# Half-size products for pairs of ff tiles in batches 1 to 3, with one set of keys and queries and a new order of steps

## The chip, the core and the metric

The kernel runs on one core of a Trainium2 chip. The core has a matrix engine (TensorE, "PE" in the profile, with its weight loads as a row of their own, "PEld"), a vector engine (VectorE, "DVE"), an activation engine (ScalarE, "ACT"), a general engine (GpSimd, "POOL") and SyncE ("SP"), which here only issues transfers. Each engine works through its own queue in order and waits on semaphores of the others. PE writes into PSUM, eight banks of 2 KB per partition; all other tiles lie in SBUF. The metric is the device time of one execution in microseconds (us), lower is better; times of several runs are given as a median. Inputs are drawn once and are the same in all runs.

## What is computed

A sparse attention followed by a two-layer network, for 4 batches of 768 positions with 8 heads of 64:

```
k_sum, v_sum = max / mean of k, v over blocks of 32 positions
scores = scale * q k^T, kept where |i - j| < 16, beside scale * q k_sum^T + log(32)
attn   = softmax(scores) [v ; v_sum]            # (4, 8, 768, 64) -> x (3072, 512)
h      = x @ w_in                               # 512 -> 2048
g      = h * sigmoid(1.702 h)
out    = g @ w_out                              # 2048 -> 512
```

## The kernel before

The program is one long list of steps, the string `ORDER`. Each word names a step with its arguments; a step calls a small function that issues the step's instructions, each on a fixed engine, and every engine runs its instructions in the order of the words (`_Ordered`, so that all instructions have line 28 in the profile). A last letter a, d or g names the engine of a step: ACT, DVE or POOL. The order is written out by hand or by a planner outside the file; there is no scheduler in it. The work of a batch:

- **Loads and keys.** `lk`, `lq`, `lv` issue the loads of keys, queries and values on POOL. For batch 0 and 1 keys and queries are turned on PE; for batches 2 and 3 `xk` and `xq` turn them by transposing transfers on SP. `xa` is DVE's maximum over key blocks, `ka` and `kR` copy halos and block rows. `kxs` and `qTs` are two sets of keys and queries, used in turn (`b % 2`); set 0 lies in the pool `even`. `vw` are two sets of values.
- **Attention.** `s` scores (PE), `e` exponent (ACT), `m` mask (DVE), `v` values (PE), `nn` normalisation (DVE). Then `d`, a transposing transfer on SP, brings x into `xTT[half][g]` (half of the positions, half of d_model). It is interleaved with the products of the batch before.
- **ff.** `f.half.nt.k0123.bank`: four matmuls of 128x128 by 128x384 add up one of 16 tiles of h for one half in a bank; `g.half.nt`: gelu on ACT into `gTb[:, nt, half]`. 32 such tiles per batch.
- **Sums and products.** The second layer is already done with half-size blocks, seven products in place of eight: `gs.j.n.w` are four kinds of sums (w = 0 to 3) of blocks of g for n tiles from j, 16-bit tensors; `ws.w.part` the same for w_out, once. `p.t.w` is product w = 1 to 7 for position tile t = 0 to 2, eight matmuls of 256 columns each. Products 1, 2 and 4 take g as it is, 5, 6, 7 and 3 take sums 0, 1, 2 and 3. `x.t.w` takes a finished product out of its bank, on ACT or DVE; `o` stores to DRAM on SP.
- **Others.** `vm`, `vb` block sums of values, `sd`, `ha` transfers of halos of values, `gate.n` a small POOL copy that holds POOL's later loads back until values of a batch are in place, `G` and `X` load ACT's tables.

Functions for seven products in the first layer exist (`w_sum7`, `x_sum7`, `product7`, `taken7`, `gelu7`), but `ORDER` calls only `P7.0`, which closes the pool `even` and opens nothing. PSUM is used as four single banks (0 to 3) and two double ones (`4x`, `5x`; a third digit 0, 1 or 2 is first half, second half or both).

Of the kernel before, what the change touches and what calls it, by code (L numbers as in the profile page):

```python
# [17 lines left out]
class _Ordered:  # L18


    def __init__(self, tc, eng):
        self._tc, self._eng = tc, eng

    def __getattr__(self, name):
        f = getattr(self._eng, name)

        def call(*a, **kw):
            r = f(*a, **kw)  # L28
            self._tc.keep_in_program_order(r)
            return r  # L30

        return call
# [23 lines left out]
qc.1.a gs.6.1.3 lv.2.0.0 tq.2.42 p.1.1.3 qc.2.a gs.7.1.1 gs.4.2.3 p.0.5.1 x.0.5.a p.0.6 tq.3.52 kr.0.1.d s.1.0.0.42
x.0.6.a x.0.2.a gs.7.1.2 X gs.7.1.3 kr.1.1.d x.1.1.d xm.3.1 kh.2.1.g p.1.2.0 e.0.0 p.0.3 p.0.7 lq.2.3 m.0.0 x.0.3.a
x.0.7.a kh.1.1.d qc.3.d s.1.1.0.42 e.1.0 p.1.6 xm.2.1 vm.1.42 o.0.0.0.0.2 s.1.0.1.52 lv.2.5.0 e.0.1 kr.2.1.g kh.3.1.d
p.0.4 vb sd.1.1.0 x.0.4.a gate.1 s.1.1.1.52 e.1.1 lv.2.3.0 p.1.5.1 kr.3.1.d x.1.5.d x.1.2.a m.1.0 x.1.6.a s.1.0.2.52
sd.1.0.0 p.2.1.2 m.0.1 x.2.1.a p.1.3 s.1.0.3.42 o.0.0.1.0.2 p.1.7 lv.2.1.1 e.0.2 m.1.1 lk.2.0 e.0.3 s.1.1.2.52 lk.2.2  # L60
lv.2.2.0 x.1.7.a x.1.3.a lv.2.2.1 lk.2.3 p.2.6 e.1.2 lv.2.5.1 s.1.1.3.42 m.0.2 p.1.4 v.1.0.0.50 e.1.3 v.1.0.1.51 lk.2.1
m.0.3 m.1.3 lk.2.4 v.1.1.0.40 v.1.1.1.41 x.2.6.a p.2.5.1 G lk.2.5 nn.0.0 nn.1.0 x.2.5.a lk.2.7 p.2.7 o.0.1.0.0.2
t.0.0.52 lk.2.6 x.2.7.a x.1.4.a p.2.2.3 t.1.0.42 p.2.3 x.2.2.a c.0.0.a c.1.0.a m.1.2 lv.2.1.0 v.1.0.2.50 lq.2.1
v.1.0.3.51 v.1.1.2.40 x.2.3.a v.1.1.3.41 p.2.4 f.0.1.k01.0 nn.0.1 t.0.1.52 nn.1.1 lv.2.0.1 c.0.1.d o.0.1.1.0.2 lq.2.4
lv.2.3.1 x.2.4.a o.0.2.0.0.2 f.0.9.k01.3 f.0.8.k01.1 f.0.0.k01.2 lv.2.4.0 t.1.1.42 c.1.1.d f.0.1.k23 g.0.1 f.0.8.k23
f.0.0.k23 g.0.8 g.0.0 f.0.9.k23 o.0.2.1.0.2 g.0.9 lq.2.6 lv.2.4.1 xk.0.0.0 lq.2.5 f.1.1.k0123.0 f.1.0.k0123.2 lq.2.7
g.1.0 xk.0.0.1 g.1.1 f.1.8.k0123.1 lv.3.1.0 xk.0.1.0 g.1.8 xk.0.1.1 f.1.9.k0123.3 f.0.2.k0123.2 g.1.9 g.0.2
f.1.2.k0123.1 lk.3.0 f.1.10.k0123.3 g.1.2 f.0.10.k0123.0 f.1.3.k0123.1 xq.0.0 gs.0.2.0 g.1.10 g.1.3 g.0.10
f.1.11.k0123.3 f.0.3.k0123.2 f.0.11.k0123.0 g.1.11 g.0.3 f.1.12.k0123.3 gs.0.2.2.d xq.0.1 g.0.11 gs.0.2.1.g
f.0.4.k0123.2 f.1.4.k0123.1 g.0.4 xa.0.0 f.0.12.k0123.0 g.1.4 f.0.5.k0123.2 f.1.5.k0123.1 g.0.12 lk.3.4 g.1.12  # L70
f.0.13.k0123.0 f.1.15.k0123.3 g.0.5 f.0.6.k0123.2 g.1.5 g.0.13 lv.3.1.1 g.1.15 vm.2.42 f.0.14.k0123.0 gs.2.2.0 ka.0.g vb
f.1.6.k0123.1 lk.3.2 g.0.14 g.0.6 lk.3.7 f.1.13.k0123.3 lk.3.3 gs.2.2.1 f.0.15.k0123.0 gs.2.2.3 lk.3.5 g.1.6 ha.2.2.0
g.1.13 f.1.7.k0123.2 f.1.14.k0123.3 lv.3.4.1 f.0.7.k0123.1 g.1.7 xa.1.0 gs.7.1.0 sd.2.0.0 kR.0.d g.0.15 lv.3.0.1
sd.2.1.0 g.1.14 gs.4.2.0 p.0.2.0 s.2.0.0.42 gs.6.1.0 ha.2.0.0 g.0.7 gs.7.1.2 s.2.0.1.52 lv.3.5.0 gs.4.2.1 X lv.3.2.0
p.2.5.1 p.0.1.2 e.0.1 gs.7.1.1 gs.7.1.3 ha.2.3.0 gs.6.1.1 x.0.1.d p.0.5.3 x.0.2.a x.0.5.d e.0.0 m.0.0 s.2.0.2.42
gs.6.1.2.d gs.6.1.3 ha.2.1.0 s.2.0.3.52 gs.4.2.2.d e.0.2 e.0.3 gs.0.2.3 p.1.5.0 p.0.6 gs.4.2.3 gs.2.2.2.d s.2.1.0.42
s.2.1.1.52 x.0.6.a lk.3.1 p.0.3 p.0.7 e.1.0 x.0.3.a lv.3.3.0 m.0.3 lq.3.0 p.1.1.3 x.0.7.a e.1.1 lq.3.4 m.0.1 s.2.1.3.52
m.0.2 s.2.1.2.42 x.1.1.a e.1.3 e.1.2 p.0.4 p.1.6 lv.3.0.0 x.0.4.a v.2.0.0.40 x.1.6.a v.2.0.2.50 v.2.0.1.41 x.1.5.d
v.2.0.3.51 m.1.2 p.1.2.2 m.1.1 lq.3.5 p.1.7 o.1.0.0.0.2 nn.0.0 x.1.2.a o.1.0.1.0.2 m.1.3 x.1.7.a p.1.3 nn.0.1 lv.3.3.1
lq.3.7 m.1.0 p.1.4 p.2.1.2 v.2.1.0.40 v.2.1.2.50 d.0.0 v.2.1.1.41 v.2.1.3.51 x.2.5.a x.2.1.d x.1.3.a lq.3.3 p.2.6  # L80
o.1.1.0.0.2 x.1.4.d d.0.1 p.2.3 nn.1.0 x.2.6.a p.2.7 nn.1.1 p.2.2.3 x.2.7.a x.2.2.a lv.3.4.0 d.1.0 lv.3.2.1 p.2.4
f.0.9.k01.3 x.2.3.a f.0.1.k01.0 G d.1.1 o.1.2.0.0.2 f.0.1.k23 f.0.8.k01.1 f.0.8.k23 f.0.9.k23 x.2.4.a f.0.0.k01.2
f.0.0.k23 lk.3.6 g.0.1 g.0.9 g.0.8 f.1.1.k0123.0 f.1.8.k0123.1 g.0.0 f.1.9.k0123.3 g.1.1 g.1.9 g.1.8 f.1.0.k0123.2
f.0.10.k0123.0 g.0.10 gate.2 g.1.0 gs.0.2.2 xk.1.1.0 f.1.2.k0123.1 gs.0.2.0.d gs.0.2.1 xk.1.0.1 f.1.10.k0123.3 g.1.2
o.1.1.1.0.2 g.1.10 lq.3.6 f.0.2.k0123.2 gs.0.2.3 lv.3.5.1 f.1.3.k0123.1 vm.3.52 g.1.3 xk.1.1.1 g.0.2 xk.1.0.0
o.1.2.1.0.2 f.0.13.k0123.0 f.0.3.k0123.2 f.1.11.k0123.3 f.0.12.k0123.1 g.0.3 g.0.13 g.1.11 xa.0.1 f.0.4.k0123.2 xq.1.1
f.1.12.k0123.3 lq.3.1 f.0.11.k0123.0 g.0.4 gs.2.2.2.g g.0.12 f.1.5.k0123.1 g.0.11 lq.3.2 vb xa.1.1 xq.1.0 f.0.5.k0123.2
# [12 lines left out]
f.1.13.k0123.3 g.1.2 f.1.3.k0123.1 g.0.10 f.0.3.k0123.2 g.1.13 f.1.10.k0123.3 g.0.3 f.0.11.k0123.0 f.0.4.k0123.2 g.1.3  # L100
# [13 lines left out]
def kernel(  # L114
# [633 lines left out]

    seven = {}

    def seven_pool(n):
        even.close()
        if not n:
            return
# [209 lines left out]
```

## Time and profile before

| | us |
|---|---|
| median of 3 runs | 212.25 |
| lowest, highest | 211.74, 213.11 |
| the profiled execution, whole | 211.7 |
| its span in the trace | 210.0 |

All rows of a profile come from the profiled execution. Its span runs from the first to the last instruction; the remaining 1.7 us lie around it. PE's mean granted clock was 0.996. Engines' busy times are unions, so pipelined instructions count once. A timeline row gives start, length, engine, line, operation, what it writes and reads, and how many like instructions are merged in it; in brackets the idle time before it and what ended it. In rows of groups, "busy, mean ns" is followed by the idle time of the engine before these instructions.

### The profile page before, as it was taken

How to read it: one execution, taken by the hardware profiler on the slowest of the kernel's cores; microseconds unless marked ns; L12 is line 12 of the kernel's file. 1: busy time of each engine (PE TensorE's matmuls, PEld its weight loads, DVE VectorE, ACT ScalarE, POOL GpSimd, SP SyncE). 2: the span in 40 equal slices, each digit the busy share in tenths (PEclk: the TensorE clock that was granted, in tenths of full speed). 3: DMA queues.
4: the chain of work that ended last, by engine and by line, in shares of the span. 5: the costliest groups of instructions: out<-in, count | busy, mean ns of one | idle time of the engine just before them, and what ended most of it. 6: DMA issues, size and time to landing. Idle time of an engine off the chain costs nothing.

```text
span 210.0 us, 5880 instructions
## 1 busy us (share of the span) xinstructions
PE 200.4 (95%) x2440; PEld 145.8 (69%) x2440; DVE 130.8 (62%) x311; ACT 114.3 (54%) x227; POOL 109.1 (52%) x157
## 2 busy tenths in 40 slices
PE   7998798999999999999999999999999999999993
PEld 5656554667887886556788865657888865668882
DVE  5577873798997871168997822694888500166342
ACT  2473885659666736676764336567670157671100
POOL 7999972399982998448949422431000000863000
PEclk9999999999999999999999999999999999999998
DMA  4999999999999999999999999939215920000214
GB/s 67 162 166 189 209 213 221 182 144 122 99 134 199 156 177 183 130 126 141 148 166 204 142 227 180 187 29 169 50 53 139 160 105 0 0 3 0 100 53 150
DMA packets 96458, 27.74 MB, mean 132 GB/s; under 512 B 85024, under 2 KB 93488, under 8 KB 96432
## 3 DMA queue, kind: packets, MB, share of 16 engines
q0 software_dynamic: 70800, 13.64, 82.7%
q1 hardware_dynamic: 25632, 13.74, 33.2%
q8 instruction: 19, 0.31, 0.6%
q14 instruction: 7, 0.06, 0.1%
HBM read 27.26 MB, written 6.29 MB: 160 GB/s over the span
## 4 chain that ended last, share of the span: by engine, by line
PE 79%; POOL 12%; DMA 5%; issue 1%; DVE 1%; SPq 0%; POOLq 0%; DVEq 0%
PE ph L28 36%; PE poA L28 19%; PE poB L28 10%; PE poC L28 5%; PE ps_s L28 3%; PE ps_av L28 3%; DMA vw<-vw 2%; POOL mk L28 2%; DMA out_dram<-osb 2%; POOL v0n L28 2%; POOL w_in_sb L28 2%; POOL kb L28 2%; POOL kx L28 2%; POOL qb L28 1%; PE ps_t L28 1%
## 5 line engine op out<-in xcount | busy, mean ns | idle before, releaser
L28 PE MATMUL ph<-xT,w_in_sb 128*128 128x384 f16 x512 | 86.1, 326 | 0.4 <-DVE osb L28 0.4
L28 ACT ACTIVATE gT<-ph 128x384 f16<-128x384 f32 x128 | 56.1, 495 | 30.6 <-PE ph L28 29.9
L28 PEld LDWEIGHTS <-w_in_sb 128*128 128x128 f16 x512 | 49.2, 98 | 32.4 <-issue 0.9
L28 PEld LDWEIGHTS <-gs 128*128 128x128 f16 x384 | 36.5, 98 | 4.6
L28 DVE TENSOR_TENSOR gs<-gT 128x768 f16<-128x768 f16 (+1 forms) x36 | 17.5, 498 | 29.1 <-ACT gT L28 29.0
L28 POOL TENSOR_TENSOR gs<-gs,gT 128x768 f16<-128x768 f16 (+1 forms) x6 | 8.8, 1461 | 41.8 <-PE ph L28 32.7
L28 POOL DMA_DIRECT2D kb<-in_k_dram x28 | 23.1, 842 | 13.7 <-DMA w_out_sb<-in_moe_w_out_dram 6.4
L28 ACT ACTIVATE a_sb<-ps_s 128x768 bf16<-128x768 f32 x32 | 24.8, 808 | 9.5 <-PE ps_s L28 9.3
L28 PEld LDWEIGHTS <-gT 128*128 128x128 f16 x288 | 27.3, 98 | 3.6
L28 POOL DMA_DIRECT2D vw<-in_v_dram x36 | 25.7, 752 | 5.0 <-DMA w_out_sb<-in_moe_w_out_dram 1.7
L28 PE MATMUL poA<-ws,gs 128*128 128x256 f16 x192 | 24.8, 273 | 0.0
L28 POOL DMA_DIRECT2D qb<-in_q_dram x28 | 23.8, 867 | 1.8 <-issue 0.9
L28 DVE TENSOR_TENSOR a_sb<-a_sb,mk 128x768 bf16<-128x768 bf16 x28 | 14.7, 550 | 3.0 <-ACT a_sb L28 2.2
L28 DVE TENSOR_TENSOR x<-ps_av,rc 128x768 f16<-128x768 f32 (+1 forms) x18 | 15.6, 869 | 0.6
L28 ACT ACTIVATE s<-poA 128x256 f32<-128x256 f32 x14 | 5.4, 382 | 19.3 <-PE poA L28 18.6
L28 PE MATMUL poB<-ws,gs 128*128 128x256 f16 x96 | 12.5, 273 | 0.0
L28 PE MATMUL poC<-w_out_sb,gT 128*128 128x256 f16 x96 | 12.5, 273 | 0.0
L28 PE MATMUL poA<-w_out_sb,gT 128*128 128x256 f16 x96 | 12.4, 273 | 0.0
L28 PE MATMUL poB<-w_out_sb,gs 128*128 128x256 f16 x96 | 12.4, 273 | 0.0
L28 PE MATMUL poA<-ws,gT 128*128 128x256 f16 x96 | 12.3, 273 | 0.0
L28 DVE TENSOR_REDUCE ka<-kx 128x48 bf16<-128x1536 bf16 x4 | 7.0, 1750 | 7.4 <-DMA kx<-kb 7.4
L28 ACT ACT_TABLE_LOAD x8 | 10.3, 1283 | 0.9 <-PEq L948 0.8
(102 smaller groups left out, 219.0 us busy)
## 6 DMA issues: line engine op xcount, KB each, us to landing
out_dram<-osb SPq DMA_DIRECT2D x23, 256.0 KB, 2.9
kb<-in_k_dram POOLq DMA_DIRECT2D x24, 96.0 KB, 6.0
qb<-in_q_dram POOLq DMA_DIRECT2D x24, 96.0 KB, 5.0
vw<-in_v_dram POOLq DMA_DIRECT2D x36, 64.0 KB, 5.1
w_out_sb<-in_moe_w_out_dram POOLq DMA_DIRECT2D x4, 512.0 KB, 14.8
w_in_sb<-in_moe_w_in_dram POOLq DMA_DIRECT2D x3, 512.0 KB, 11.3
vw<-vs SPq DMA_DIRECT2D x6, 198.0 KB, 3.9
kb<-in_k_dram POOLq DMA_DIRECT2D x4, 192.0 KB, 4.4
```

The source lines that it names most:

```text
L28: r = f(*a, **kw)
```

## The change

The first layer is done with seven half-size products for some pairs of ff tiles (j, j + 8): pairs 2 to 4 in batches 1 and 2, and 2 to 7 in batch 3 (the sums of w_in for pairs 5 to 7 are made between, in batch 2's ff and products). The others stay as they are. For a pair, with a11, a12 (rows 0 to 255 and 256 to 511 of w_in for tile j), a21, a22 (the same for tile j + 8) and b11, b12, b21, b22 (x: upper or lower half of d_model, first or second half of positions):

- `W.w.j.n` are four kinds of sums of the blocks a for n pairs from j, `U.w` four of the blocks b, once per batch.
- `P.j.w` is product w, two matmuls of 384 columns. Product 1 opens the first half of a double bank (`phX`, "l"), product 5 the second ("r").
- `S.j.1` copies product 1 from l into a single bank (`phA`), on which products 6, 7 and 4 are then added up; product 2 is added on l. `S.j.5` copies product 5 into an SBUF tile h. `S.j.6` writes phA + h back into r, on which product 3 is added; `S.j.7` writes phA + h into h.
- `H.j.0`, `H.j.1`, `H.j.2` are the gelus: of l and r together (768 columns), of phA, and of h.

So the accumulators are seeded by an engine's write into PSUM and later products are added there. Before, `taken7` (unused) copied to SBUF and added there.

Further: batches 1 to 3 share set 1 of keys and queries (`min(b, 1)`), and the pool of set 0 is closed early in batch 0 (`P7.6.2`), where the tiles of the seven products take its place; both sets of values move to the pool `keep`. Sum 2 of g (`gs.j.n.2`) is written over the right half of `gTb` in place, which makes the tile of sums a quarter smaller. `mask` and `w_sum` can be given an engine; masks, sums and copies of keys are spread anew over DVE and POOL, and the order of steps from the ff of batch 0 on is written anew.

```diff
...
+            if self._last is not None:
+                self._tc.add_manual_dep(r.ins, self._last, mybir.DependencyInfo(
+                    mybir.DependencyClass.NoSync, mybir.DependencyReason.DATA), reason="program order")
+            self._last = r.ins.name
...
-    vw = [sets[s].tile([128, NQ, H, VC], BF16, name=f"vw{s}") for s in range(2)]
+    vw = [keep.tile([128, NQ, H, VC], BF16, name=f"vw{s}") for s in range(2)]
...
-        score_tiles(st["S", half, p], p, b % 2, half)
+        score_tiles(st["S", half, p], p, min(b, 1), half)
...
-    def mask(half, p):
+    def mask(half, p, eng=dve):
...
+        p7 = ctx.enter_context(tc.tile_pool(name="seven", bufs=1, side="right", reuse_waits="tile"))
+        seven["pool"], seven["j0"] = p7, j0
+        seven["w"] = p7.tile([128, 4, 2, n * 128], F16, name="ws7", tag="ws7")
+        seven["x"] = p7.tile([128, 4, 2, HALF], F16, name="xs7", tag="xs7")
...
+        if where is not None:
+            X = seven[j, "X"] = bank(where, F32, "phX")
+            seven[j, "l"], seven[j, "r"] = X[:, 0:HALF], X[:, 512:512 + HALF]
         for i in range(2):
+            pe.matmul(out=seven[j, name], lhsT=lhs[:, i], rhs=rhs[:, i], start=(what in (1, 5) and i == 0),
+                      stop=(i == 1), skip_group_check=True)
+
+    def taken7(j, what, eng, where=None):
+
+        if what == 1:
+            seven[j, "A"] = bank(where, F32, "phA")[:, 0:HALF]
+            copy(eng, seven[j, "A"], seven[j, "l"])
+        elif what == 5:
+            seven[j, "h"] = seven["pool"].tile([128, HALF], F32, name="r7", tag="r7", bufs=3)
+            copy(eng, seven[j, "h"], seven[j, "r"])
         else:
+            to = seven[j, "r"] if what == 6 else seven[j, "h"]
+            eng.tensor_tensor(out=to, in0=seven[j, "A"], in1=seven[j, "h"], op=ALU.add)
...
+        o, i = ((gTb[:, j].rearrange("p (h c) -> p h c", h=2),
+                 lambda: seven[j, "X"].rearrange("p (h c) -> p h c", h=2)[:, :, 0:HALF]),
+                (gTb[:, k2, 0:HALF], lambda: seven[j, "A"]), (gTb[:, k2, HALF:S], lambda: seven[j, "h"]))[which]
...
-        gs = snap.tile([128, 4, NT // 2, HALF], F16, name="gs")
+        t3 = snap.tile([128, 3, NT // 2, HALF], F16, name="gs")
+        gs = [t3[:, 0], t3[:, 1], gTb[:, 0:NT // 2, HALF:S], t3[:, 2]]
...
```

The new order, where the steps stand of which the prediction speaks: a stretch of batch 2's ff, then the last half of batch 3's ff and its joint with the products.

```
...
S.3.7.d S.4.5.a P.4.2 xa.0.1 P.4.6 P.3.3 g.1.6 ka.1.d P.3.4 H.3.2 S.4.6.d f.0.6.k0123.2 g.0.14 H.3.0 lq.3.2 f.1.13.k0123.3
...
H.5.0 gs.2.2.0.d gs.2.2.1.d P.6.5 H.4.1 S.6.5.d P.7.1.52 S.6.1.a.0 P.7.5 f.1.0.k0123.2 S.7.5.d H.5.1 g.0.9 P.6.6
gs.2.2.3 g.1.0 S.7.1.a.1 P.6.2 f.1.9.k0123.3 S.6.6.d P.7.2 o.2.2.1.0.2 P.7.6 P.6.3 S.7.6.d P.6.7 P.7.3 H.5.2 g.1.9 P.7.7
H.6.0 S.6.7.d S.7.7.d H.7.0 P.6.4 H.6.1 H.6.2 gs.0.2.0.d p.0.1.2 gs.0.2.1.d H.7.2 gs.4.2.0.g gs.0.2.3.d gs.6.1.0.d
gs.4.2.1 gs.6.1.1 gs.7.1.0 gs.2.2.2.g gs.6.1.2.d P.7.4 gs.7.1.1.d H.7.1 gs.4.2.3 x.0.1.a gs.0.2.2.g p.1.1.3 gs.6.1.3
gs.7.1.2 gs.7.1.3.d p.0.2.0 p.0.5.1 p.0.6 x.0.5.a x.0.6.a gs.4.2.2.g p.0.3 x.0.2.a p.0.7 x.0.7.a p.2.2.0 p.0.4 x.0.3.a
...
```

In the old order batch 3's ff is 32 tiles `f` with their gelus, and its sums stand between them; two products of batch 2 (`p.2.7`, `p.2.4`) that stood before that ff stand inside it now, behind its first tiles.

More of the change, by code (lines that the diff above doesn't have):

```diff
@@ L21, in __init__ @@
     def __init__(self, tc, eng):
-        self._tc, self._eng = tc, eng
+        self._tc, self._eng, self._last = tc, eng, None
     def __getattr__(self, name):
@@ L58 @@
[L58 to L62, printed above, removed]
@@ L83 @@
[L83 to L87, printed above, removed]
@@ new lines @@
+f.0.0.k23 f.0.9.k23 U.0.d lq.3.5 lv.3.3.1 lq.3.7 lq.3.3 lv.3.4.0 g.0.0 g.0.1 P.3.1.52 g.0.9 lv.3.2.1 P.2.5 lk.3.6
+f.1.0.k0123.2 f.1.1.k0123.0 U.2.d S.2.5.d f.1.8.k0123.1 W.0.5.3.d f.1.9.k0123.3 o.1.2.0.0.2 g.1.0 g.1.8 U.1.g g.1.1
+P.3.5 gate.2 xk.1.1.0 U.3.g xk.1.0.1 f.0.8.k01.1 S.2.1.a.0 lq.3.6 f.0.8.k23 P.2.2 P.2.6 g.1.9 f.0.13.k0123.2
+f.0.15.k0123.3 S.2.6.d P.2.7 S.3.5.d lv.3.5.1 g.0.13 f.0.5.k0123.2 g.0.15 g.0.8 f.1.5.k0123.3 P.2.3 lq.3.1 gs.0.2.0.d
+g.1.5 S.3.1.d.1 S.2.7.d H.2.0 P.3.6 P.3.2 f.1.14.k0123.3 o.1.1.1.0.2 S.3.6.d gs.0.2.1.g P.2.4 g.0.5 P.4.1.42 P.3.7 P.4.5
@@ L744, in g_sums, with seven_pool @@
         a1l, a1r, a2l, a2r = gTb[:, j, l], gTb[:, j, r], gTb[:, k2, l], gTb[:, k2, r]
-        a, b, op = ((a1r, a2r, ALU.add), (gs[:, 0, j], a1l, ALU.subtract), (a1l, a1r, ALU.subtract),
-                    (a2l, gs[:, 1, j], ALU.subtract))[what]
-        eng.tensor_tensor(out=gs[:, what, j], in0=a, in1=b, op=op)
+        a, b, op = ((a1r, a2r, ALU.add), (gs[0][:, j], a1l, ALU.subtract), (a1l, a1r, ALU.subtract),
+                    (a2l, gs[1][:, j], ALU.subtract))[what]
+        eng.tensor_tensor(out=gs[what][:, j], in0=a, in1=b, op=op)
     seven = {}
-    def seven_pool(n):
+    def seven_pool(n, j0=0):
         even.close()
@@ L786, in product7 @@
             4: (w_in_sb[:, 2:4, d], x[:, 3], "A")}[what]
-        opens = where is not None
-        if opens:
-            seven[j, name] = bank(where, F32, "ph" + name)[:, 0:HALF]
-        seven[j, "at", what] = ph = seven[j, name]
+        if where is not None:
+            X = seven[j, "X"] = bank(where, F32, "phX")
+            seven[j, "l"], seven[j, "r"] = X[:, 0:HALF], X[:, 512:512 + HALF]
         for i in range(2):
-            pe.matmul(out=ph, lhsT=lhs[:, i], rhs=rhs[:, i], start=(opens and i == 0), stop=(i == 1),
-                      skip_group_check=True)
@@ L795, in taken7 @@
-    def taken7(j, what, eng):
-        ph = seven[j, "at", what]
-        if what in (1, 6, 5):
-            if what == 1:
-                seven[j, "h"] = seven["pool"].tile([128, 2, HALF], F32, name="h7", tag="h7")
-            if what == 5:
-                seven[j, "r"] = seven["pool"].tile([128, HALF], F32, name="r7", tag="r7")
-            copy(eng, {1: lambda: seven[j, "h"][:, 0], 6: lambda: seven[j, "h"][:, 1],
-                       5: lambda: seven[j, "r"]}[what](), ph)
-        else:
-            t_ = {2: lambda: seven[j, "h"][:, 0], 3: lambda: seven[j, "h"][:, 1], 7: lambda: seven[j, "r"]}[what]()
-            dve.tensor_tensor(out=t_, in0=ph, in1=t_, op=ALU.add)
+            pe.matmul(out=seven[j, name], lhsT=lhs[:, i], rhs=rhs[:, i], start=(what in (1, 5) and i == 0),
+                      stop=(i == 1), skip_group_check=True)
@@ L814, in gelu7, with w_sum @@
         act.activation(out=o, in_=i(), func=ACT.Gelu_apprx_sigmoid)
     N1 = d_model // 2
-    def w_sum(what, part):
+    def w_sum(what, part, eng=dve):
         n = NT // 2
@@ L824, in w_sum @@
         a, b = {0: (b12, b11), 1: (b22, ws[:, 0, c]), 2: (b22, b12), 3: (b21, ws[:, 1, c])}[what]
-        dve.tensor_tensor(out=ws[:, what, c], in0=a, in1=b, op=ALU.subtract)
+        eng.tensor_tensor(out=ws[:, what, c], in0=a, in1=b, op=ALU.subtract)
     now = {}
@@ L856, in taken @@
             name = {1: "s1", 6: "s2", 5: "s5"}[what]
-            p_ = seven.get("pool", snap) if what == 1 else snap
-            t_ = now[t, name] = p_.tile([128, N1], F32, name=name, tag=name)
+            t_ = now[t, name] = snap.tile([128, N1], F32, name=name, tag=name)
             copy(eng, t_, po)
```

154 lines of the change are left out of this document (75 added, 79 removed).

## The prediction

> **What bounds the kernel now.** I read the page's totals first, then busy time by stage, then what PE waited for, then the chain of waits, and last single instructions at the joints between stages.
>
> ```profile
> span 210.0 us, 5880 instructions
> ...
> PE 200.4 (95%) x2440; PEld 145.8 (69%) x2440; DVE 130.8 (62%) x311; ACT 114.3 (54%) x227; POOL 109.1 (52%) x157
> ```
>
> ```profile
> core 0: us, PE busy (x) PEld busy (x) DVE busy (x) ACT busy (x) POOL busy (x), PEclk, DMA share, GB/s
> ...
> 78.00:99.50 21.50, 21.50 (x183) 13.12 (x181) 10.29 (x15) 13.80 (x31) 14.28 (x18) 1.00 2.02 152
> 99.50:123.00 23.50, 22.75 (x360) 19.20 (x359) 19.51 (x47) 11.76 (x20) 14.65 (x20) 1.00 1.84 173
> 123.00:145.10 22.10, 22.00 (x201) 13.22 (x200) 12.84 (x26) 13.83 (x33) 6.70 (x7) 1.00 0.93 147
> ...
> 167.20:188.10 20.90, 20.90 (x131) 12.61 (x129) 3.75 (x6) 13.56 (x31) 8.32 (x5) 1.00 0.09 29
> 188.10:206.60 18.50, 18.30 (x168) 16.16 (x166) 9.37 (x24) 2.79 (x7) 1.82 (x2) 1.00 0.17 63
> ```
>
> These stages are the ff of batch 1; the products of batch 1 with the attention of batch 2; the ff of batch 2; the ff of batch 3; the products of batch 3. PE is full in each, at full clock, and the other engines have room in the ff stages. What PE waited for after 50 us:
>
> ```profile
> PE ps_s L28 <- issue: 0.4, 1, 0.4
> PE ph L28 <- DVE osb L28: 0.4, 1, 0.4
> ```
>
> So each matmul less is time saved, as long as no new wait takes its place.
>
> **What goes.** The chain of waits holds the ff of batch 3 and a product behind it in unbroken pieces (start, length, count):
>
> ```profile
> 167.26 20.80 PE ph L28 x128
> 188.06 0.87 PE poA L28 x8
> ```
>
> A matmul of 384 columns costs 20.80 / 128 = 0.1625 us, one of 256 columns 0.109. A pair of ff tiles took 2 tiles x 2 halves x 4 = 16 matmuls and takes 7 x 2 = 14; twelve pairs save 24 x 0.1625 = **3.9 us**, 1.95 of it in batch 3. At 123 us the first ff tile waited 0.4 for DVE to read a bank; now P.2.1 and half a tile in other banks (0.65 us) come first, and this 0.4 goes too.
>
> **What comes.** The nearest rows:
>
> ```profile
> L28 ACT ACTIVATE gT<-ph 128x384 f16<-128x384 f32 x128 | 56.1, 495 | 30.6 <-PE ph L28 29.9
> ...
> L28 DVE TENSOR_TENSOR a_sb<-a_sb,mk 128x768 bf16<-128x768 bf16 x28 | 14.7, 550 | 3.0 <-ACT a_sb L28 2.2 <-POOL mk L28 0.7
> ...
> L28 POOL TENSOR_TENSOR gs<-gT 128x768 f16<-128x768 f16 x4 | 6.5, 1634 | 6.9 <-ACT gT L28 6.9
> ...
> L28 DVE TENSOR_TENSOR osb<-poA,s 128x256 f32<-128x256 f32 x12 | 5.1, 422 | 3.7 <-PE poA L28 3.7
> ...
> L28 DVE TENSOR_TENSOR x<-ps_av,rc 128x384 f16<-128x384 f32 x4 | 2.2, 558 | 0.1
> ```
>
> ```profile
> 102.68 0.36 DVE L28 TENSOR_TENSOR gs<-gT,gs 128x384 f16<-128x384 f16 x1
> 102.96 0.35 DVE L28 TENSOR_TENSOR gs<-gs,gT 128x384 f16<-128x384 f16 x1
> ```
>
> ```profile
> 130.05 1.03 DVE L28 TENSOR_TENSOR gs<-gT 128x768 f16<-128x768 f16 x2 [6.67 <-ACT gT L28]
> ```
>
> The gelus stay: a pair had four of 384 columns and has one of 768 and two of 384. New are four evictions a pair (S): 48 of 128x384 from PSUM. The trace has none that writes PSUM; the bounds are 0.42 (the 256-column add) and 0.63 (0.42 x 384 / 256), and I take 0.56, the row with 384 columns read from PSUM. New sums on DVE, 128x768 in 16 bit, cost 1.03 / 2 = 0.51 in a row; those of 384 columns start 0.28 apart; on POOL 1.63 each.
>
> Batch 1, the tightest stage: DVE has 10.3 busy of 21.5; 12 evictions (6.7), four U and three W (3.6) come, two sums (1.0) leave for POOL: 19.6 of 20.5. No more than full, and most products have other tiles' matmuls between one eviction and the matmul that needs it; I charge 0.3 for latencies. DVE's key reductions (xa) now have evictions queued behind them, and PE behind those; they wait for transposed keys:
>
> ```profile
> 90.75 1.75 DVE L28 TENSOR_REDUCE ka<-kx 128x48 bf16<-128x1536 bf16 x1 [5.92 <-DMA kx<-kb]
> ```
>
> In the new order DVE reaches this step behind S.4.6, by PE's count about 14 us into the stage, at about 92.8: 2 us after the keys came. Cover, then, of 2 us. The single set of keys adds no wait that shows: batch 2's keys were fetched in this same stage, after batch 1's last scores. SP issues the same transfers in the same order between its neighbours. Seven_pool moves into batch 0, behind the last score that reads the old set; it issues nothing itself. In the attention stages nine masks go from DVE (0.55) to POOL (1.63), two of them in front of the POOL instruction that gates the loads of batch 2; I charge 0.3 for what waits there, bounds 0 and 1.6 (one mask).
>
> **The joint at the end of batch 3** decides. Counted from P.3.1, PE has 116 matmuls of 384 columns (18.85) and two products left from batch 2 (1.74); all but P.7.4 are issued at 20.3, or 20.45 with 0.15 of latencies in the last two pairs. P.7.7 is out at 20.1, its result 0.16 later, S.7.7 then ends at 20.85. The products of tile 0 follow: p.0.1 and p.1.1 and p.0.2 (0.87 each) and P.7.4 (0.33) need no sums and keep PE busy to 23.4. Then p.0.5 wants the sums gs.0, whose last slice, gs.7.1.0, its eighth matmul reads, at 24.15. That a product starts before its last sum exists is seen in the old joint:
>
> ```profile
> 188.77 1.04 PE L28 MATMUL poB<-ws,gs 128*128 128x256 f16 x8
> 189.00 0.36 DVE L28 TENSOR_TENSOR gs<-gT 128x384 f16<-128x384 f16 x1 [0.22 <-ACT gT L28]
> ```
>
> Behind S.7.7 DVE has, in order, gs.0.2.0, 0.2.1, 0.2.3, 6.1.0, 4.2.1, 6.1.1 and 7.1.0: 4 x 0.51 + 3 x 0.28 = 2.9, ready at 23.75, 0.4 early. But POOL runs its sums gs.4.2.0 (from about 18.2, when ACT is through with H.5.2), 2.2.2, 0.2.2 and 4.2.2 at the same time. What the two engines do to each other:
>
> ```profile
> 92.42 1.71 DVE L28 TENSOR_TENSOR gs<-gT 128x768 f16<-128x768 f16 x1
> ```
>
> ```profile
> 92.06 1.65 POOL L28 TENSOR_TENSOR gs<-gs,gT 128x768 f16<-128x768 f16 x1
> ```
>
> ```profile
> 185.37 0.49 DVE L28 TENSOR_TENSOR gs<-gT 128x384 f16<-128x384 f16 x1 [6.01 <-ACT gT L28]
> 185.79 1.99 DVE L28 TENSOR_TENSOR gs<-gs,gT 128x768 f16<-128x768 f16 x1
> ```
>
> ```profile
> 184.01 1.63 POOL L28 TENSOR_TENSOR gs<-gT 128x768 f16<-128x768 f16 x1
> 185.61 1.76 POOL L28 TENSOR_TENSOR gs<-gs,gT 128x768 f16<-128x768 f16 x1
> ```
>
> A DVE sum of 0.5 us took 1.71 and 1.99 where a POOL sum ran, and ended 0.4 after it. In the second case POOL's sum came in between two DVE sums that stood back to back. So in the new joint gs.2.2.2 (19.85 to 21.5) holds gs.0.2.0 back by 0.65, and gs.0.2.2 and gs.4.2.2 (1.65 each) get in between DVE's sums: gs.7.1.0 comes at 23.75 + 3.95 = 27.7, and PE stands 27.7 - 24.15 = 3.5 us; with 0.2 at p.0.3, whose sums come last, 3.7. The bounds are 0 (DVE keeps its turn) and 3.95; I take 3.7, by the event at 185.6.
>
> The Trainium skill bears on this in "SBUF — State Buffer", section "Who interferes with whom": VectorE and GpSimd share one pair of SBUF ports under an exclusive lock, the engine that starts first keeps it for its whole instruction, and a VectorE instruction with at most one SBUF input isn't concerned. The rows above agree (1.71 for 0.51); by its last clause the evictions, which read PSUM and at most one tile of SBUF, go free, which no row here proves for 384 columns. If the engines shared bandwidth instead, the sum would be nearer the lower bound.
>
> **The sum.** On the profiled execution, 211.7 (span 210.0 and 1.7 around it): 211.7 - 3.9 - 0.4 + 3.7 + 0.3 + 0.3 = 211.7. The median of the three runs is 212.25, 0.55 higher. The two gains and the unseen bounds lean downwards, so for the median I say 211.9.
>
> **Rivals.** *DVE keeps its turn at the last joint* (or PE reaches it with more slack than I count): the 3.7 falls away, 212.25 - 4.3 + 0.6 = 208.6, and up to 209.8 if one POOL sum still gets in. For it: one event is thin evidence for who goes first. Against: in both collisions shown DVE waited out POOL's whole instruction.
>
> *Late keys, slower.* If POOL's masks and sums push back the loads of keys, DVE stands at xa with evictions behind it, and PE at the next accumulation. It decides from 2 us on, the cover above; with the keys 4 us later in batches 1 and 2 it costs 2 x 2 = 4 us beside the joint's 3.7: 215.9. For it: POOL's two masks and two key copies more before the gate, which opens here at 67.04 after a wait of 4.16, so that most of them fit in that wait:
>
> ```profile
> 67.04 0.18 POOL L28 COPY gate<-vw 32x1 bf16<-32x1 bf16 x1 [4.16 <-DMA vw<-vs]
> ```
>
> Against it: that same wait.
>
> *The change does not do what it says*: excluded for the matmuls (the built program has 24 fewer); the time can only be given back elsewhere.
>
> **How the numbers follow.** POOL in between (211.9, itself 210.3 to 213.4): 0.45. DVE keeps its turn: 0.37. Late keys: 0.18. One per cent, about what a measurement of this kernel can tell from no change, is 210.1 to 214.4. Faster: all of the second case and a tail of the first, 0.40. Within: 0.42. Slower: the third case but for its mild part, with a tail of the first, 0.18. The range reaches from the middle of the second case's time to the beginning of the third's: 208.5 to 214.4.
>
> **What would show it.** PE rows 24 fewer. In the ff stages of batches 1 and 2, no PE wait on phA, phX or r over 0.3. At the last joint, one PE or weight-load wait on a gs sum of about 3.5, with DVE sums of 1.5 to 2 us beside POOL's gT sums; if DVE's sums there last 0.5 and PE does not wait, the second case holds. DVE idle before ka with a wait of phX behind it would be the third. I am wrong altogether if evictions into PSUM last over 0.65, or if PE stalls in the new order of batch 0, where I have charged nothing but the masks.

## The result and the profile after

The changed kernel takes 226.92 us (median of 4 runs, 225.61 to 227.29) beside 212.0 us for the kernel before (4 runs, 211.42 to 213.11): a ratio of 1.069, interval 1.062 to 1.075. It is 14.5 us slower by the ratio, and outside the predicted range. Differences in us between runs are below those of the ratios before rounding, times 212 us, because a ratio leaves out single disturbed executions, which a median still holds.

The page of the changed kernel, its span, totals and rows of slices (tenths of busy time in 40 slices, last the granted clock):

```profile
span 225.2 us, 5942 instructions
...
PE 201.3 (89%) x2416; PEld 144.2 (64%) x2416; DVE 155.6 (69%) x335; ACT 119.5 (53%) x231; POOL 147.5 (65%) x185
...
PE   7997899999998999997799699669799999986993
...
POOL 7999943699999895988779579157653190191000
PEclk9999999999999999999999999979999999996999
```

PE has the 24 rows fewer that were forecast (2416 for 2440), yet is busy for 0.9 us longer: the clock was lowered twice (7 and 6 in the last row), which is a large part of it. DVE rose from 130.8 to 155.6 us, POOL from 109.1 to 147.5.

Where the time went is read from the start of PE's first product or first ff matmul in each stage:

| stage begins at, us | before | after | difference |
|---|---|---|---|
| products of batch 1 | 99.32 | 98.56 | -0.8 |
| ff of batch 2 | 123.10 | 124.45 | +1.4 |
| products of batch 2 | 145.09 | 153.16 | +8.1 |
| ff of batch 3 | 167.10 | 175.85 | +8.8 |
| products of batch 3 | 187.90 | 198.07 | +10.2 |
| last matmul ends | 206.4 | 221.6 | +15.2 |

Busy time by stage in the changed kernel (products 1, ff 2, ff 3 and products 3 answer to the rows shown of before; the first row is the ff of batch 1):

```profile
core 0: us, PE busy (x) PEld busy (x) DVE busy (x) ACT busy (x) POOL busy (x), PEclk, DMA share, GB/s
78.00:98.50 20.50, 20.50 (x184) 12.50 (x177) 16.65 (x30) 13.88 (x29) 17.46 (x22) 1.00 1.81 160
98.50:124.40 25.90, 23.09 (x362) 19.22 (x360) 20.26 (x40) 12.53 (x22) 21.85 (x24) 1.00 1.17 130
124.40:153.10 28.70, 22.59 (x173) 12.84 (x171) 14.96 (x28) 13.82 (x30) 16.66 (x18) 0.94 1.26 140
175.80:198.00 22.20, 21.25 (x132) 12.69 (x131) 13.51 (x27) 14.22 (x28) 8.40 (x6) 1.00 0.20 36
198.00:221.60 23.60, 20.67 (x172) 17.06 (x170) 13.88 (x27) 4.49 (x12) 5.18 (x3) 0.93 0.11 38
```

PE is full in the first row only. Six us of the ff of batch 2 and 2.9 of the last products are idle. What PE waited for (us in total, times, longest):

```profile
PE phX L28 <- DVE phX L28: 3.5, 1, 3.5
PE poB L28 <- DVE gs L28: 2.8, 2, 2.1
PE phX L28 <- DVE xs L28: 2.4, 2, 2.0
PE poA L28 <- DVE gT L28: 1.6, 1, 1.6
PE poB L28 <- DVE s L28: 1.5, 1, 1.5
```

The first wait is one for late keys and the third one for x, which came late by transfer; before the other three, DVE was held. **POOL holds DVE.** In the products of batch 1 a mask on POOL, not a sum, lay beside two DVE sums of 0.35 us each:

```profile
106.01 2.05 DVE L28 TENSOR_TENSOR gT<-gT 128x384 f16<-128x384 f16 x2
```

```profile
106.14 1.70 POOL L28 TENSOR_TENSOR a_sb<-a_sb,mk 128x768 bf16<-128x768 bf16 x1 [0.79 <-ACT a_sb L28]
```

DVE's two sums ended 0.2 us after POOL's mask, and product 7 waited 1.64 us for them. (Before the fifth wait, two sums on DVE took 3.37 us from 156.25 on, beside sums on POOL.) **Loads stand behind POOL's masks.** In the same stage POOL waited for exponents (8.2 us in five places over the whole run), and the loads behind it waited too; the last load of keys was issued at 125.99 us (116.74 before). In the ff of batch 2 DVE's key maximum came to stand with an eviction behind it:

```profile
145.26 1.75 DVE L28 TENSOR_REDUCE ka<-kx 128x48 bf16<-128x1536 bf16 x1 [4.26 <-DMA kx<-kb]
...
147.50 0.56 DVE L28 TENSOR_TENSOR phX<-phA,r 128x384 f32<-128x384 f32 x1
```

```profile
148.11 0.48 PE L28 MATMUL phX<-xT,ws 128*128 128x384 f16 x2 [3.48 <-DVE phX L28]
...
150.29 2.71 PE L28 MATMUL ph<-xT,w_in_sb 128*128 128x384 f16 x8
```

PE stands 3.48 us, and afterwards eight matmuls that otherwise take 1.46 us take 2.71: **the clock was lowered after the wait.** The last joint looks as forecast:

```profile
202.11 1.78 DVE L28 TENSOR_TENSOR gs<-gT 128x384 f16<-128x384 f16 x1
```

```profile
199.76 3.92 POOL L28 TENSOR_TENSOR gT<-gT 128x768 f16<-128x768 f16 x2 [0.49 <-DVE gs L28]
```

```profile
203.94 0.35 PE L28 MATMUL poB<-ws,gs 128*128 128x256 f16 x1 [2.11 <-DVE gs L28]
204.95 0.40 PE L28 MATMUL poB<-ws,gs 128*128 128x256 f16 x1 [0.66 <-DVE gs L28]
205.14 1.91 PE L28 MATMUL poA<-ws,gs 128*128 128x256 f16 x8
```

### The profile page after: what moved, and what is told of

It is laid out like the page before. It is cut to its first block, busy times and chain, and to the rows that moved or that the text cites. A ratio compares the mean times of both kernels' runs of the same rounds, so it can differ in the third digit from the quotient of the medians.

```text
span 225.2 us, 5942 instructions
## 1 busy us (share of the span) xinstructions
PE 201.3 (89%) x2416; PEld 144.2 (64%) x2416; DVE 155.6 (69%) x335; ACT 119.5 (53%) x231; POOL 147.5 (65%) x185
## 5 line engine op out<-in xcount | busy, mean ns | idle before, releaser
L28 PE MATMUL ph<-xT,w_in_sb 128*128 128x384 f16 x320 | 60.4, 331 | 0.9 <-DMA xT<-x 0.6
L28 PEld LDWEIGHTS <-w_in_sb 128*128 128x128 f16 x392 | 37.8, 99 | 26.4 <-issue 3.0
L28 ACT ACTIVATE gT<-ph 128x384 f16<-128x384 f32 x80 | 36.7, 492 | 31.8 <-PE ph L28 31.7
L28 PEld LDWEIGHTS <-gT 128*128 128x128 f16 x384 | 36.4, 98 | 7.8 <-DVE gT L28 2.3
L28 PEld LDWEIGHTS <-gs 128*128 128x128 f16 x288 | 28.0, 100 | 9.9 <-DVE gs L28 3.9
L28 PE MATMUL poA<-ws,gT 128*128 128x256 f16 x192 | 25.3, 273 | 1.9 <-DVE gT L28 1.6
L28 POOL DMA_DIRECT2D qb<-in_q_dram x28 | 23.5, 848 | 0.1
L28 POOL TENSOR_TENSOR a_sb<-a_sb,mk 128x768 bf16<-128x768 bf16 x9 | 15.5, 1736 | 8.2 <-ACT a_sb L28 8.2
L28 PEld LDWEIGHTS <-ws 128*128 128x128 f16 x96 | 9.4, 97 | 13.6 <-issue 7.7
L28 POOL TENSOR_TENSOR xs<-xT,xs 128x768 f16<-128x768 f16 x4 | 6.8, 1705 | 12.6 <-DVE xs L28 8.5
L28 PE MATMUL poA<-ws,gs 128*128 128x256 f16 x96 | 13.3, 285 | 1.1 <-DVE s L28 1.1
```

## The experiments

All runs are on one core beside runs of the kernel before on the same chip. Theory: POOL's new work (masks and sums) makes the loss, by holding DVE and by delaying loads. Main rival: the seven half-size products themselves, with their evictions and latencies. A cut from the order shows the changed words alone, which need not stand side by side there.

**e1: POOL's masks and sums back on DVE.** Nine masks and 24 sums, of which one of each kind is shown; loads and copies of keys stay on POOL.

```diff
-m.0.1.g gs.0.2.0.g U.1.g W.1.5.3.g
+m.0.1   gs.0.2.0   U.1.d W.1.5.3.d
```

> The changed kernel with all nine masks and all of POOL's sums (of g, of x and of w_in) back on DVE; POOL keeps loads and copies of keys. Theory (POOL's tensor work does the harm, by holding DVE's two-input instructions and by making POOL's loads late): the waits of PE on gs, gT and s at the joints (7.4 us in the changed kernel), on late keys and late x (6.3) and the lower clock after them (about 3) go, 226.9 - 16.7 = 210 us, up to 213 with 22 more instructions on DVE. Rival (the products themselves do it: chains from PE to DVE and back, a DVE that is too full): 222 or more, with PE waits on phA, phX and r in the ff stages.

Measured 217.01 us, ratio 1.022 (1.017 to 1.026). Two thirds of the loss, 10.0 us, were POOL's masks and sums. But 4.6 us remain, more than the theory allowed (213 us at most): the rival has a part too, though its number (222 or more) is as far off.

**e2: only the nine masks back.**

```diff
-m.0.1.g m.0.0.g m.0.0.g m.0.3.g m.1.3.g m.1.2.g m.1.0.g m.1.2.g m.1.3.g
+m.0.1   m.0.0   m.0.0   m.0.3   m.1.3   m.1.2   m.1.0   m.1.2   m.1.3
```

> The changed kernel with only the nine masks back on DVE. If the masks in POOL's queue make the loads of the next batch late (theory of the late loads), the waits on keys (3.5) and on x in the ff of batch 2 (2.6) go with their clock loss (1.5), and two of the holds: about 218. If the lock between POOL's sums and DVE is what counts, only the masks' own two holds (1.6 and less) go: 224 to 225. If the products themselves do it: no change.

220.63 us, ratio 1.042 (1.036 to 1.047): 5.7 us less, between what theory and rival expected. The wait for keys is gone.

**e3: only the 24 sums back.** The other half of e1's edit.

> The changed kernel with only POOL's sums back on DVE, the masks stay on POOL. If the lock counts, the holds at the joints go (2.8 and its clock loss 1.1 at the last, 1.5 in the products of batch 2, 1.1 in those of batch 1): about 220. If the late loads count more, POOL is free 2.8 us earlier in the products of batch 1, and the wait for keys shrinks by that: about 219 together with the first, but the waits on x stay. If the products themselves do it: no change or slower.

222.83 us, ratio 1.049 (1.044 to 1.055): 4.1 us less, where 219 to 220 us were expected, 7 to 8 less. The masks seem worse than the sums (the intervals of e2 and e3 overlap), and 5.7 + 4.1 is about e1's 10.0, so the two act side by side.

**e4: the kernel before, with the same nine masks on POOL.**

```diff
-    def mask(half, p):
+    def mask(half, p, eng=dve):
         a = a_sb[half, p]
-        dve.tensor_mul(a, a, mk[:, half * TH:(half + 1) * TH, :].unsqueeze(1)
+        eng.tensor_mul(a, a, mk[:, half * TH:(half + 1) * TH, :].unsqueeze(1)
```

> The kernel before, with the same nine masks put on POOL where they stand, and nothing else. Late loads: the keys of batch 3 come some 6 to 9 us later than before, but behind DVE's key reductions there are only sums here: 212 + 1 to 3 us. The lock alone: holds of up to 1.2 us each on masks and sums of DVE, most of them beside PE work: 212 + 0 to 2. If POOL masks cost nothing without the products: 212 within 0.5.

216.25 us, ratio 1.018 (1.013 to 1.022), beside 212.06: the masks alone cost 3.8 us in the old order, above what was expected (at most 3). PE's two longest new waits (from its timeline):

```profile
109.25 1.08 PE L28 MATMUL poB<-w_out_sb,gs 128*128 128x256 f16 x8 [1.41 <-DVE gs L28]
127.52 2.11 PE L28 MATMUL ph<-xT,w_in_sb 128*128 128x384 f16 x12 [1.65 <-DMA xT<-x]
```

The second is a wait for x, whose last three transposes start at 120.99 us in place of 118.58. The last load of keys is later too (122.98 us for 116.74), but PE waits for no keys here. The first is a DVE sum that lasted 2.74 us beside a mask of 1.72:

```profile
105.99 2.74 DVE L28 TENSOR_TENSOR gs<-gT 128x768 f16<-128x768 f16 x1
```

```profile
106.58 1.72 POOL L28 TENSOR_TENSOR a_sb<-a_sb,mk 128x768 bf16<-128x768 bf16 x1
```

**e5: the four sums ahead of the last products on DVE.** This isolates the forecast 3.7 us.

```diff
-gs.4.2.0.g gs.2.2.2.g gs.0.2.2.g gs.4.2.2.g
+gs.4.2.0.d gs.2.2.2.d gs.0.2.2.d gs.4.2.2.d
```

> The changed kernel with only the four sums of g that POOL makes ahead of the last products (gs.4.2.0, gs.2.2.2, gs.0.2.2, gs.4.2.2) given to DVE; all else as it was. Theory (POOL's sums hold DVE's sums there, as the prediction had it): product 5 no longer waits 2.11 and 0.66 us at 204 to 205 us, and the products behind it run at the full clock again (about 1 us): 226.9 - 2.8 - 1.0 = 223.1 us, range 222 to 224.5. Rival (the sums are late because too many of them stand between the last gelus and the products, on whichever engine; four more on DVE at some 0.6 to 1.2 us each take the place of the lock): 226 to 228 us, with PE's wait at product 5 as long as before.

223.23 us, ratio 1.052 (1.044 to 1.060): 3.5 us less, in the theory's range. DVE does four sums more and is through sooner:

```profile
204.58 0.28 PE L28 MATMUL poB<-w_out_sb,gs 128*128 128x256 f16 x1 [0.27 <-DVE gs L28]
205.11 0.28 PE L28 MATMUL poB<-w_out_sb,gs 128*128 128x256 f16 x1 [0.25 <-DVE gs L28]
```

The last stage, from its first product to the last matmul's end, shrank from 23.5 to 20.2 us (18.5 before), and every product in it lasts about 1.04: in this execution the lowered clock went with the wait.

**e6: the last two key loads ahead of the masks.**

```diff
+lk.3.1 lk.3.6
 m.0.0.g lv.3.0.1
...
-lk.3.1
...
-lk.3.6
```

> The changed kernel with the last two loads of batch 3's keys (lk.3.1, lk.3.6) put ahead of the masks in POOL's queue in batch 2's scores (where the first of the four stands), all else as it was. Theory (keys come late because their last load stands behind POOL's masks, issued at 125.99 us): the transposes of keys start at about 127 to 128 us in place of 134.6, DVE's maximum no longer waits 4.26 us, PE's 3.48 us wait at 148 us falls to under 0.5, and some 1 us of lowered clock behind it goes: 226.9 - 3.3 - 1.0 = 222.6 us, range 221.5 to 224. Rival (SP's transposes are late because x of batch 2 and the sums behind the gate are late, whatever the loads do): the transposes still start after 132 us, 225.5 to 227.5 us.

224.93 us, ratio 1.061 (1.051 to 1.071). The mechanism is as the theory has it: the transposes of keys start at 126.48 us in place of 134.62, and the wait of 3.48 us is gone, with the slow eight matmuls behind it:

```profile
126.48 3.85 SPq L28 DMA_TRANSPOSE kx<-kb  x2
```

The gain is 1.7 us, not the 4.3 expected, and its interval overlaps the changed kernel's. The clock was lower instead: the means of the four executions are 0.969 to 0.977 beside 0.983 to 0.992, and in the profiled one it was 0.93 in the products of batch 1. Nor is 3.48 us the wait's fixed size: in e5, whose steps are those of the changed kernel up to there, it was 1.11 us.

**e7: the six pairs of batch 3 undone.** e1, and from batch 3's ff on the words of the kernel before (ordinary `f` and `g` for `P`, `S`, `H`; no `U`, no `W` for pairs 5 to 7).

> The kernel with masks and sums back on DVE (217.0 us), and from batch 3's ff on the order of the kernel before: its six pairs are ordinary tiles again, their sums of w_in and x are not made, batches 1 and 2 keep three pairs each. Twelve matmuls of 0.164 us come back, 1.97 us. Theory (six pairs with few ordinary tiles between leave PE waiting on evictions, some 2.3 us in that ff, and delay the last joint by some 1.7): 217.0 + 2.0 - 4.0 - up to 0.8 for DVE's sums of w_in in batch 2's products = 214.5 us, range 213.5 to 215.5. Rival (the pairs of batch 3 pay what they save and the loss in e1 lies elsewhere): 218 to 219.5 us.

215.07 us, ratio 1.014 (1.006 to 1.021). With twelve matmuls more it is 1.7 us quicker than e1. The theory's number (214.5, at most 215.5) holds; the rival's (218 and up) falls. In e1 that ff shows small waits and none that is large:

```profile
175.02 0.48 PE L28 MATMUL phA<-xs,ws 128*128 128x384 f16 x2 [0.19 <-DVE phA L28]
176.42 0.48 PE L28 MATMUL phX<-xT,ws 128*128 128x384 f16 x2 [0.26 <-DVE phX L28]
181.53 0.48 PE L28 MATMUL phA<-xs,ws 128*128 128x384 f16 x2 [0.26 <-ACT phA L28]
```

**e8: batch 2's pairs undone too.** The same from batch 2's ff on.

> As the run before, but from batch 2's ff on the order of the kernel before (with the set of keys shared and sums 0 ahead of sums 2, which are written in place): only batch 1's three pairs are left. Theory (three pairs save what was forecast, 0.98 us, and what is lost in batch 1's products, 1.9 us by the starts of the stages with masks and sums on DVE, comes from the order of steps there and stays): 212.1 - 1.0 + 1.9 = 213.0 us, range 212.3 to 214. Rival (that loss has slack behind it at the gate, and the saving arrives): 210.5 to 211.6 us. Second rival (sharing one set of keys makes keys late by itself): 215 us or more, with a wait for keys at 145 us.

213.24 us, ratio 1.006 (1.002 to 1.010). Again quicker, by some 1.6 us, with six matmuls more. The theory's range (212.3 to 214) holds. The second rival (keys late by the shared set) falls: no such wait is left.

**e9: batch 1's products in the old order too.** Only batch 0 and batch 1's ff keep the new order.

> As e8 (pairs of batch 1 alone, masks on DVE), but the order of the kernel before is taken up already at the start of batch 1's products, with its sums, masks and loads where they stood; only batch 0 and batch 1's ff keep the new order. Theory (three pairs save 0.98 us and the stage of products behind them, 23.8 us in the kernel before and some 26.4 in e8, is longer by its new order of steps alone): 212.1 - 1.0 + 0.2 = 211.3 us, range 210.6 to 212.0. Rival (the stage behind is longer because the ff ahead of it ends with sums and evictions of the pairs still to come, whatever follows): 212.8 to 213.6 us, with PE waits on DVE in the products at 99 to 124 us.

Ratio 1.010 (1.006 to 1.014), 213.87 us: the theory (211.3) falls, and the time is just above the rival's (212.8 to 213.6). The ff ends 1.5 us earlier than before (first product at 97.79), and the scores then wait for DVE:

```profile
100.71 0.53 PE L28 MATMUL ps_s<-qT,kx 64*128 64x64 bf16 x24 [1.89 <-DVE vs L28]
```

The queries that the scores need came no earlier, though: SP had issued their transposes by 98.63 us, and by 97.23 before.

**e10: the same with pairs in batches 1 and 2.**

> Pairs in batches 1 and 2, three each, in the new order of their two ff stages; products of both batches and all of batch 3 in the order of the kernel before, masks on DVE, no sums of w_in for pairs 5 to 7. Theory (the seven products pay where an ff has three pairs among ordinary tiles, and the loss comes from what was moved around them): 212.1 - 1.97 + 0.5 for the second batch's sums of x and latencies = 210.6 us, range 209.8 to 211.8. Rival (each ff with pairs gives its saving back in the products behind it): 213 to 214.5 us.

Ratio 1.014 (1.008 to 1.020), 214.3 us: the theory falls here too. Waits for DVE's sums of values and rows of keys stand behind each ff with pairs, 2.53 us at 101.46 and 1.11 at 147.68.

**e11: values and key rows ahead of the sums of g.** e9, with

```diff
-xa.1.1 gs.4.2.0 lk.3.4 P.3.4 kR.1.d H.3.2
+xa.1.1 vm.2.52 kR.1.d vb gs.4.2.0 lk.3.4 P.3.4 H.3.2
...
-vm.2.42
...
-vb
...
-s.2.0.0.42
+p.0.1.2 s.2.0.0.42
```

> e9 with DVE's work at the end of batch 1's ff in another order: the block sums of values (vm, in the other double bank, and vb) and the key rows (kR) go ahead of the four sums of g that stood before them, and the second first-half product ahead of the first scores. Theory (the 1.89 us that PE waits for scores at 100.7 us is DVE's queue, sums of g and evictions of pairs ahead of the sums of values, and the later transfers of halos follow from it): that wait falls under 0.5 us, the waits for halos at 113 us from 1.5 to about 0.8, and the time by 1.5 to 2: 213.9 - 1.8 = 212.1 us, range 211.2 to 212.8, no faster than the kernel before. Rival (SP's transposes of queries, 10.7 us of issue, set the scores and the halos): no change, 213.4 to 214.4 us.

Ratio 1.011 (1.007 to 1.016), 213.89 us: no gain, the number of the rival (213.4 to 214.4: SP's transposes set the scores), though the wait for scores is gone from the trace. Another came in its place, a product that waits for DVE to read its bank:

```profile
104.88 1.03 PE L28 MATMUL poB<-ws,gs 128*128 128x256 f16 x8 [1.82 <-DVE osb L28]
```

So one step of DVE's queue was not the cause. Either the queue as a whole was late, or SP's transfers were; this run doesn't part the two. (The profiled execution was the quickest of the six, 211.83; the trace shows less loss than the median has.)

**e12: the same order in e10**, and kR.1 of batch 2 right behind xa.1.1.

> e10 with the same for batch 1's ff, and in batch 2's ff the key rows (kR) right behind the second key maximum, ahead of the sums of g. Theory: the waits of 2.53 us at 101.5 and 1.11 us at 147.7 fall under 0.5 each, halos come earlier: 214.3 - 1.9 - 0.8 = 211.6 us, range 210.6 to 212.6, about the kernel before and at best 1 us under it. Rival (keys and queries on SP set both places): 213.5 to 215 us.

Ratio 1.015 (1.010 to 1.019), 214.42 us: no gain either, the rival's number again, with 1.82 us for DVE at 107.63.

**e13: no pairs; one set of keys, sum 2 in place.** The kernel before with the two small changes alone.

```diff
-        score_tiles(st["S", half, p], p, b % 2, half)
+        score_tiles(st["S", half, p], p, min(b, 1), half)
...
-xk.0.0.0 xk.0.0.1 xk.0.1.0 xk.0.1.1 xq.0.0 xq.0.1 xa.0.0 xa.1.0 kR.0.d ka.0.g
+xk.1.0.0 xk.1.0.1 xk.1.1.0 xk.1.1.1 xq.1.0 xq.1.1 xa.0.1 xa.1.1 kR.1.d ka.1.g
```

> No pairs at all: the order of the kernel before, with only two things of the change: batches 1 to 3 share one set of keys and queries, and sum 2 of g is written in place (so that sum 0 goes ahead of it). Theory (neither costs anything, the keys' transposes start after the scores anyway, and what is left in e8, e9 and e11 is the pairs): 212.0 us, range 211.4 to 212.6. Rival (the shared set holds the transposes of the next batch's keys back, or a sum that must wait for its operand costs the products): 213 to 214 us, which would be all that e9 loses.

Ratio 1.004 (1.001 to 1.007), 211.9 us beside 211.28: in the range expected, but not nothing, 0.3 to 1.4 us. Which of the two it is, no run says.

**e14: e9 without its pairs.** New order up to batch 1's ff, then the order of before.

> As e13, and the new order of steps up to the start of batch 1's ff (masks and sums of it on DVE, no sums of w_in), then the order of before; no pairs. It is e9 without its pairs. Theory (the pairs of batch 1 cost what e9 has over the kernel before): 212.0 us, range 211.4 to 212.8. Rival (the new order of batch 0 costs it): 213.5 to 215 us.

Ratio 1.010 (1.006 to 1.013), 212.82 us beside 211.28: some 1.2 us (1.010 for 1.004) come from the new order of batch 0. The number stands between theory (at most 212.8) and rival (213.5 and up). In the trace PE waits 1.74 us at 124.86 for DVE, where it waited 0.41 before, and SP's three transposes of x, issued from 119.02 on, took 6.01 us (3.91 before). e9, which has three pairs on top, stands at the same 1.010: six matmuls less bought nothing that shows there.

**e15: batch 1's pairs with as little around them as could be.** Batch 0 and all stages from batch 1's products on in the old order, the end of that ff as in e11, the sums of w_in at its start.

> The pairs of batch 1 alone with the least around them: the order of the kernel before in batch 0, in batch 1's products and after, the new order in batch 1's ff only, DVE's end of that ff in the order of e11; one key set and sums in place as in e13 (1.004 of the kernel before). The sums of w_in stand at the start of batch 1's ff. Theory (six matmuls of 0.164 us less arrive when DVE is not late behind that ff): e13 less 0.98, so 0.9995 of the kernel before, 211.2 to 212.0 us where that is at 211.7. Rival (a saving in that ff is given back in the products behind it, because keys, queries and halos of the next batch come at the same time as before): 1.004 or more, 212.5 us and up.

Ratio 1.005 (1.001 to 1.009): the rival's number, and e13's without pairs (1.004). The trace shows how the saving is given back in the profiled execution, first in waits and then by the clock:

```profile
97.28 1.04 PE L28 MATMUL poC<-w_out_sb,gT 128*128 128x256 f16 x8
98.99 0.58 PE L28 MATMUL ps_s<-qT,kx 64*128 64x64 bf16 x12 [0.68 <-POOL kx L28]
100.49 0.35 PE L28 MATMUL ps_s<-qT,kx 64*128 64x64 bf16 x12 [0.92 <-DVE vs L28]
100.77 0.39 PE L28 MATMUL poB<-ws,gs 128*128 128x256 f16 x2
101.55 0.93 PE L28 MATMUL poB<-ws,gs 128*128 128x256 f16 x6 [0.39 <-DVE gs L28]
102.27 1.91 PE L28 MATMUL poA<-w_out_sb,gT 128*128 128x256 f16 x8
103.98 1.81 PE L28 MATMUL poB<-ws,gs 128*128 128x256 f16 x8
```

The products start 2.04 us earlier than before (99.32), more than the 0.98 of the six matmuls, then wait 0.68 + 0.92 + 0.39 = 1.99 us for key rows, sums of values and sums of g, and two products of 1.04 us then take 1.91 and 1.81. The clock can't be the whole of it: six other executions had it at 1.00 throughout and took 211.25 to 215.07 us.

No run with pairs had a ratio below 1.

## Why the prediction was wrong

The forecast was 211.9 us, in a range of 208.5 to 214.4; "slower" had 0.18.

- **The 24 matmuls.** They went, and where nothing else stood in the way they went from the time: the ff of batch 1 ends 0.8 us earlier in the changed kernel. The step "each matmul less is time saved, as long as no new wait takes its place" failed by its condition. With POOL's work taken away, undoing batch 3's pairs gained 1.7 us (e7) and batch 2's 1.6 (e8), and batch 1's were worth nothing that shows (e9 beside e14, e15 beside e13). The intervals of e1, e7 and e8 overlap at their ends, and each of the last two comparisons is good to about 1 us, which is what three pairs should save (0.98), so these sizes are rough. In all of them the order of steps changes with the pairs.
- **Latencies, 0.3 in batch 1 and 0.15 in batch 3.** The first is right for the ff itself. What the step left out is the stage behind: DVE was counted as "no more than full" (19.6 of 20.5 us, measured 16.65), but its sums of values, key rows and sums of g for the next stage come last in its queue, and PE now gets there sooner. The second is too small: batch 3's six pairs cost the 1.95 us that they save and the 1.7 that their undoing gave back in e7, with all that goes with them. A good part stands behind the ff: the last products take 20.3 us in e1 (from 190.53) and 18.5 in e7 (from 191.20).
- **Masks, 0.3 with bounds of 0 and 1.6.** The largest error. Taking the nine masks off POOL gave 5.7 us in the changed kernel (e2), and putting them into the kernel before cost 3.8 (e4). The prediction priced only what waits at one gate. It had the rule for sums, that POOL's instruction holds a DVE sum, and did not apply it to masks; and its sum held nothing for loads queued behind masks that wait for exponents (they stood in the third case alone).
- **POOL's sums elsewhere.** Also charged at nothing outside the last joint. All sums together gave 4.1 us (e3), 3.5 of it by e5's measure from that joint; e3 and e5 overlap, so little is left for the others when the masks stay.
- **The last joint, 3.7.** Right in kind and place: waits of 2.11 and 0.66 on a sum, beside POOL's sums of 1.64 to 1.96 us. The size agrees in part by luck: the waits are 2.8 us of it, and some 1.4 were the clock, which had no term; e5 took 3.5 away.
- **Late keys, the third case.** It came true in one of its two batches. "Against it: that same wait" took the gate of batch 1 as cover; the masks that matter stand in batch 1's products, behind that gate. The wait was 3.48 us in the one trace (1.11 in e5's), and a kernel without it some 1.7 us quicker (e6).
- **Evictions, 0.56.** Right: 0.56 and 0.57 into PSUM, as in the row at 147.50 above. The page "SBUF — State Buffer" of the Trainium skill, section "Who interferes with whom", says that a VectorE instruction with at most one SBUF input, outside the modes that use both of its port pairs, isn't held by GpSimd; the prediction left that condition out. The changed kernel's trace agrees: beside POOL sums an eviction with one input from PSUM and one from SBUF lasts 0.56 us, and a sum with two inputs from SBUF 1.52.

```profile
131.75 1.52 DVE L28 TENSOR_TENSOR ws<-w_in_sb 128x768 f16<-128x768 f16 x1
...
182.94 0.56 DVE L28 TENSOR_TENSOR phX<-phA,r 128x384 f32<-128x384 f32 x1
```

```profile
130.94 1.91 POOL L28 TENSOR_TENSOR xs<-xT,xs 128x768 f16<-128x768 f16 x1 [4.12 <-DMA xT<-x]
...
182.53 1.64 POOL L28 TENSOR_TENSOR xs<-xT,xs 128x768 f16<-128x768 f16 x1
```

- **The clock.** No term in the sum. The changed kernel ran at 0.50 from 149.42 to 152.83 us, behind the wait of 3.48, and from 204.03 to 207.44, behind and around those of 2.11 and 0.66. At half the clock, half of PE's busy time there is loss: an estimate of 1.7 and 1.4 us.

```profile
149.42:152.83 3.41, 3.41 (x58) 1.77 (x58) 3.31 (x9) 2.07 (x4) 2.79 (x4) 0.50 0.21 37
204.03:207.44 3.41, 2.75 (x13) 1.81 (x14) 3.01 (x10) 0.73 (x2) 0.00 (x0) 0.50 0.00 0
```

What stays open: why e11's and e12's medians didn't follow the removed wait (the other executions have no trace), and what in the new order of batch 0 costs the 1.2 us of e14. That DVE's late queue is what takes back the pairs' saving is read from the traces of e9, e11 and e15, each with another wait on DVE in that place; a version with that work taken from DVE wasn't tried. The rival that SP's transfers come no earlier stands untested beside it: its numbers held in e11, e12 and e15.

## What to carry to other kernels

When PE is the full engine and another engine has room, room as an average is not enough: what that engine and the transfers make ready for the next stage must come earlier by as much as the stage shrinks, or the saving turns into a wait. Work with two SBUF operands that is moved to POOL can hold DVE's own two-operand work for up to POOL's whole duration where they meet, masks like sums, and what is queued behind it on POOL, loads above all, comes later; price each such instruction at every place, not at one gate. Price a wait of PE of a few us with the clock behind it.

## What the runs showed of the hardware

The clock fell after waits that were short. In e15 no single wait in the stretch ahead was over 0.92 us, and still:

```profile
97.00:102.00 5.00, 2.96 (x41) 1.94 (x40) 4.79 (x12) 3.41 (x6) 5.00 (x9) 1.00 1.94 164
102.00:106.00 4.00, 4.00 (x38) 2.68 (x37) 3.44 (x10) 0.40 (x1) 4.00 (x6) 0.57 1.87 165
106.00:125.00 19.00, 18.66 (x301) 15.82 (x294) 15.11 (x34) 8.40 (x15) 8.72 (x12) 1.00 2.36 165
```

PE was busy for 2.96 of 5 us, and the granted clock then was 0.57 for 4 us, in which PE did not wait at all: about 1.7 us. The Trainium skill, "TensorE: Matmul & The Clock Gate", section "HAM oscillation — how this bites in real kernels", gives as its rule that idle gaps over some 3.4 us lower the clock. Here gaps that add up to 2 us in a stretch of 5 did, so short waits can't be left out of the account. But such waits don't always do it. In e2 PE was busy for 1.56 of 4.50 us, the rest being one wait of 2.94, and the clock stayed at 1.00:

```profile
153.00:157.50 4.50, 1.56 (x18) 1.44 (x15) 4.22 (x8) 1.44 (x3) 0.99 (x1) 1.00 0.02 4
157.50:160.90 3.40, 3.40 (x52) 2.78 (x50) 2.96 (x7) 1.51 (x2) 0.00 (x0) 1.00 0.20 77
```

What decides between the two cases, these runs don't show.
